# A head's two chunks on the partition halves: new layout, k loaded once, Gram in quarters, placed inverses in two buffers

## The chip, the cores and the metric

One core of a Trainium2 chip runs the whole program. The metric is the device time of one execution in microseconds; the time before is the median of three runs. A span is the part of an execution that the profile covers.

## The reference, cut to what is computed

A delta-rule attention over 4 batches, 8 heads, 768 tokens, head size 48, and two expert layers that take its output. The change touches the attention alone.

```python
k_n = k / (norm(k) + 1e-6)
for t in range(S):                       # state: 48 x 48 per batch and head
    y[t] = q[t] @ state
    state += beta[t] * outer(k_n[t], v[t] - k_n[t] @ state)
x = y as 3072 tokens x 384
x = moe(x, modality bias)                # 8 experts, the best one per token
return moe2(x)                           # 8 experts, 384 tokens each
```

## The kernel before

The tokens are cut into 24 tiles of 128, six per batch. A tile is two chunks of 64 tokens for each of 8 heads, so 16 units of 64 x 64. The recurrence in a chunk becomes a triangular inverse and a few products per unit; between chunks only the state is handed on.

Work per tile runs in three streams that the program orders by hand; each engine works through its own instructions in program order.

- Stage A, eight tiles ahead (`SLOTS = 8`): transposes of k and q (`a_trans`, L208) from the tiles kt and qt, copies to KQ (`a_copy`, ScalarE), Gram products (`a_gram`, L232) into two PSUM tiles pg, the mask times beta (`a_mask`), and the copy of the 32 x 32 diagonal blocks to Dc (`a_diag`). A half of a mask is either four VectorE instructions (L243), or four on ScalarE (L241) and one multiply by the mask on GpSimd (L247). `kbeta` (L198, GpSimd) scales k.
- Stage B, per group of four tiles (`stage_b`): VectorE transposes Dc (L271), inverts the 32 x 32 blocks by 30 substitution steps of a multiply (L282) and an add (L286), and transposes the results to XN (L290) and XTc (L292). It is a generator; `bs(k)` takes k steps of it between other VectorE work, by the tables NB0, NB1, MB and PB.
- Stage C, for tile n: `place` copies the four diagonal quarters of the inverses from XTc to XT (four DMAs on SP, L300), `join1` (L314) and `join2` (L326, copies L329) add the off-diagonal block, `solve` (L343) multiplies k and v, `prod` (L357) and `psub` (L361, VectorE) make the operators Rb, and `chain` (L383) applies them to the state, chunk after chunk, a tile later. `store` sends the result out.

The loop body for tile n runs, in this order: chain(n-1, 0), the masks of tile n+7, qcopy and chain_out, a_diag and kbeta of tile n+7, at every fourth tile a new stage B, at every third the norms of three tiles (`norm_sum`, a square root on ScalarE, `norm_fin`), bs, solve(n), chain(n-1, 1), a_trans(n+8), prod and psub for c = 0, place(n+1), join1(n+1), prod and psub for c = 1, store(n-1), bs, a_gram(n+8, 0), join2(n+1), a_gram(n+8, 1). At the end of every third tile k and v of three tiles are loaded, 10 to 12 ahead.

Before, a partition half holds one head of a pair, and a unit is a head pair in a chunk. The rows of k and v lie in RK, twelve slots; a load of some tiles is eight DMAs (four pairs by two halves, L138). k comes a second time in token order, as kt, for the transposes (L127). There is one XT, a block-diagonal 128 x 128 per unit, so that `place(n+1)` has to follow solve(n).

SP issues nearly all transfers from one queue, in program order; a wait in front of one holds those behind it. The place is:

```python
if n + 1 < NT:
    self.place(n + 1)
    self.join1(n + 1)
...
if n % 3 == 2 and n + 10 < NT:
    self.load_k(n + 10, 3, [self.nc.sync])
    self.load_v(n + 10, 3, [self.nc.sync])
```

In tiles with n % 4 = 0 the masks of the group's last tile are made: the first half on VectorE, the second on ScalarE and GpSimd; its diagonal copies are four ScalarE instructions (L265), and stage B for the group follows at once.

## Time and profile before

| | before |
|---|---|
| time, median of 3 runs | 948.79 us (948.7 to 949.35) |
| profiled execution | 950.61 us, its span 948.70 |
| TensorE busy | 821.5 us, 87% |
| VectorE busy | 641.2 us, 68% |
| ScalarE busy | 445.0 us, 47% |
| GpSimd busy | 282.5 us, 30% |
| mean granted clock of TensorE | 0.941 of full |

In the rows PE is TensorE, PEld its weight loads, DVE VectorE, ACT ScalarE, POOL GpSimd and SPq SyncE's queue of transfers. L300 is line 300 of the kernel before. Busy time of PE is modelled at its ends, so a busy PE is not a PE at its peak. A row of the timeline gives start and length in us, then, in brackets, how long the engine had been idle and what released it.

### The profile page before, as it was taken

To read this page: it belongs to the slowest core of one execution; us is meant where nothing else is said; L and a number is where in the kernel's file an instruction comes from. 1 tells how busy PE (TensorE), PEld (TensorE's weight loads), DVE (VectorE), ACT (ScalarE), POOL (GpSimd) and SP (SyncE) were. 2 spreads that over 40 slices of the span, in tenths; PEclk is the share of its full clock that TensorE was granted. 3 is DMA by queue.
4 is the path that set the end of the run, shared out by engine and by line. 5 is a ranking of instruction groups with operands and counts; after the bars stand their busy time and mean duration, and the time that the engine had idled before them with its cause. 6 is when DMAs were issued, how large, how long until landed. Compare 5 with 4: busy or idle time off the path is not lost. (4 is left out here: it accounts for less than half of the span.)

```text
span 948.7 us, 23825 instructions
## 1 busy us (share of the span) xinstructions
PE 821.5 (87%) x9415; PEld 731.8 (77%) x9415; DVE 641.2 (68%) x1744; ACT 445.0 (47%) x953; POOL 282.5 (30%) x401
## 2 busy tenths in 40 slices
PE   5659759677798886999999999987999999897996
PEld 4548658566687775699999999864778888796996
DVE  4997969787797957665744555227877867776531
ACT  3647647485667556345445554220343243233431
POOL 6254212222221012521122221123363354343411
PEclk9778979797889899999999999999999999998999
DMA  9553345444621115563185431302254235314600
GB/s 157 99 103 59 69 86 93 90 83 78 116 54 37 34 45 167 180 215 125 35 284 184 150 102 43 143 28 92 69 179 161 89 110 176 131 55 166 201 26 28
DMA packets 179402, 102.92 MB, mean 108 GB/s; under 512 B 140838, under 2 KB 161349, under 8 KB 179285
## 3 DMA queue, kind: packets, MB, share of 16 engines
q1 hardware_dynamic: 172564, 81.26, 33.3%
q0 software_dynamic: 6720, 20.07, 6.7%
q8 instruction: 77, 1.26, 0.6%
q14 instruction: 41, 0.33, 0.1%
HBM read 82.36 MB, written 14.55 MB: 102 GB/s over the span
## 5 line engine op out<-in xcount | busy, mean ns | idle before, releaser
L1083 PE MATMUL ph<-xT,HL 128*128 128x384 f32 x1152 | 232.8, 345 | 10.9 <-DVE hh L1091 8.4
L1103 PE MATMUL po<-HL,hh 128*128 128x384 f32 x1152 | 239.3, 346 | 0.2 <-DVE hh L1091 0.2
L1083 PEld LDWEIGHTS ph<-xT,HL 128*128 128x128 f32 x1152 | 202.6, 190 | 21.1 <-DVE hh L1091 10.8
L1103 PEld LDWEIGHTS po<-HL,hh 128*128 128x128 f32 x1152 | 198.0, 189 | 3.1 <-DVE hh L1091 0.5
L1086 ACT ACTIVATE hh<-ph 128x384 fp32r<-128x384 f32 x128 | 62.8, 491 | 183.1 <-PE ph L1083 156.8
L1054 DVE TENSOR_TENSOR HL<-raw,HL 128x768 fp32r<-128x768 f32 x104 | 106.5, 1035 | 56.0 <-ACT HL L1053 55.5
L1091 DVE SCALAR_TENSOR_TENSOR hh<-ph,hh 128x384 fp32r<-128x384 f32 x128 | 70.7, 553 | 80.3 <-ACT hh L1086 69.7
L1053 ACT ACTIVATE HL<-raw 128x768 fp32r<-128x768 f32 x128 | 103.3, 839 | 32.5 <-DMA raw<-in_moe_w_dram 32.4
L282 DVE TENSOR_TENSOR Dtmp<-Dt 128x30 f32<-128x30 f32 (+22 forms) x199 | 81.2, 416 | 3.9
L343 PE MATMUL pz<-RK,XT 64*64 64x96 f32 x768 | 50.2, 284 | 37.9 <-DMA XT<-XTc 36.7
L361 DVE TENSOR_TENSOR R<-pz,C 112x448 f32<-112x448 f32 x96 | 57.2, 615 | 29.7 <-PE pz L357 22.3
L286 DVE TENSOR_TENSOR Dt<-Dt,Dtmp 128x30 f32<-128x30 f32 (+22 forms) x199 | 74.8, 383 | 3.1
L343 PEld LDWEIGHTS pz<-RK,XT 64*64 64x64 f32 x768 | 43.8, 162 | 41.5 <-issue 34.8
L383 PE MATMUL pc<-SI,R 112*48 112x56 f32 (+1 forms) x1536 | 62.5, 234 | 10.8 <-DVE R L361 6.9
L383 PEld LDWEIGHTS pc<-SI,R 112*48 112x48 f32 (+1 forms) x1536 | 55.2, 143 | 18.7 <-DVE R L361 7.4
L1054 POOL TENSOR_TENSOR HL<-raw,HL 128x768 fp32r<-128x768 f32 x24 | 46.7, 1952 | 63.2 <-ACT HL L1053 63.1
L402 POOL COPY xt<-LG 128x8 f32<-128x8 f32 x24 | 5.1, 211 | 189.9 <-issue 77.2
L1141 POOL DMA_INDIRECT x2buf<-x,pidx x24 | 23.8, 993 | 106.0 <-ACT x L1137 86.0
L232 PE MATMUL pa<-KQ 64*64 64x128 f32 x640 | 47.9, 297 | 7.4 <-ACT KQ L221 7.4
L357 PE MATMUL pz<-AT,Z 64*112 64x112 f32 x768 | 50.8, 273 | 3.1 <-ACT Z L347 3.0
L357 PEld LDWEIGHTS pz<-AT,Z 64*112 64x112 f32 x768 | 42.4, 177 | 7.6 <-ACT Z L347 3.0
L232 PEld LDWEIGHTS pa<-KQ 64*64 64x64 f32 x640 | 38.7, 146 | 10.9 <-ACT KQ L221 8.1
(406 smaller groups left out, 1213.7 us busy)
## 6 DMA issues: line engine op xcount, KB each, us to landing
raw<-in_moe_w_dram SPq DMA_DIRECT2D x68, 768.0 KB, 6.0
xbuf<-xt SPq DMA_DIRECT2D x24, 196.0 KB, 1.9
qt<-in_q_dram SPq DMA_DIRECT2D x22, 192.0 KB, 3.9
kt<-in_k_dram SPq DMA_DIRECT2D x21, 192.0 KB, 3.5
RK<-in_k_dram SPq DMA_DIRECT2D x48, 72.0 KB, 2.7
RK<-in_v_dram SPq DMA_DIRECT2D x48, 72.0 KB, 2.7
XT<-XTc SPq DMA_DIRECT2D x92, 32.0 KB, 2.2
Dc<-AT SPq DMA_DIRECT2D x48, 32.0 KB, 1.9
```

What stands on the lines that cost most here:

```text
L232: nc.tensor.matmul(pg[r, p], KQ[:, 0:64], KQ, start=True, stop=True)
L282: nc.vector.tensor_mul(t[:, i:k], X[:, j + 1 + i:j + 1 + k, j:j + 1].to_broadcast([128, k - i, j]), X[:, j:j + 1, :j].to_broadcast([128, k ...
L286: nc.vector.tensor_add(X[:, j + 1 + i:j + 1 + k, :j], X[:, j + 1 + i:j + 1 + k, :j], t[:, i:k])
L343: nc.tensor.matmul(pz[r, p], self.XT[0][r, u, r], self.RK[r, n % RSLOTS, u], start=True, stop=True)
L357: nc.tensor.matmul(self.pr[h][:, p], self.Z[r, u], self.AT[r, n % SLOTS, u, 64:176], start=True, stop=True)
L383: nc.tensor.matmul(self.pc[r, hd], self.Rb[n % 2][0:112, hd % 2, c, hd // 2, r], SI[0:112, hd], start=True, stop=True)
L1053: nc.scalar.activation(t[:, i, 0, c], self.raw[s][i][:, c], AF.Copy)
L1054: (nc.gpsimd if pool else nc.vector).tensor_sub(t[:, i, 1, c], self.raw[s][i][:, c], t[:, i, 0, c].bitcast(F32))
L1083: nc.tensor.matmul(self.ph, W[:, i, a, c], x[:, k, b], start=(k == 0 and n == 0), stop=(k == 2 and n == 2))
L1086: nc.scalar.activation(h[:, 0], self.ph, AF.Relu)
L1091: self.nc.vector.scalar_tensor_tensor(h[:, 1], ph, 0.0, h[:, 0].bitcast(F32), op0=OP.max, op1=OP.subtract)
L1103: nc.tensor.matmul(self.po[s][t], h[:, a, r], W[:, 2 + i, b, c], start=(f == 0 and n == 0), stop=(f == 7 and n == 2))
```

## The change

RK is laid out by token: partition 64c + j is token j of chunk c, and a slot holds k of eight heads, each padded from 48 to 64, and behind them v. So k is loaded once, a tile per DMA, and its slot serves the transposes too; kt goes, qt gets four buffers. beta comes in one DMA. A unit is now a head, its two chunks on the two halves. The two PSUM tiles of Gram belong to the two heads of a pair; each call of `a_gram` makes two head pairs in all four quarters of the array (row half by head, column half by chunk). `psub`'s halves are chunks, so that `chain(n, 0)` reads what both calls of `psub` wrote. XT keeps only the diagonal 64 x 64 of each unit, in two buffers, and `place(n+1)` moves to the start of tile n, unless n % 4 = 3. k and v of tile n + 12 are loaded at the end of every tile. With n % 4 = 0 both halves of the mask are made on VectorE (SPH) and the diagonal copies too (DIA 2, L259). The rest of the diff follows the layout in other access patterns and isn't shown.

```diff
@@ -22,10 +22,11 @@
 NG = 6
 SLOTS = 8
 RSLOTS = 12
+QB = 4
 NB0, NB1 = (7, 8, 8, 30), (3, 6, 0, 3)
 NBT, NBS = 9, 6
 MB, PB = (0, 1, 2, 1), (1, 1, 1, 2)
-SPL, DIA, QO = (0, 0, 1, 0), (0, 3, 3, 3), (0, 1, 1, 1)
+SPL, SPH, DIA, QO = (0, 0, 1, 0), (0, 1, 1, 1), (2, 3, 3, 3), (0, 1, 1, 1)
 WM = (30, 2, 3)
 HB = 60
 NP = (4, 7, 6)
@@ -47,15 +48,16 @@
         self.ps = ctx.enter_context(tc.tile_pool(name="attp", bufs=1, space=PSUM))
         self.ident = consts["ident"]
         self.mask = cA.tile([128, 128], F32, name="mask")
+        self.K = lambda sl, cnt=1: self.RK[:, sl:sl + cnt, 0:512].rearrange("p s (u d) -> p s u d", d=64)
+        self.V = lambda sl, cnt=1: self.RK[:, sl:sl + cnt, 512:896].rearrange("p s (u d) -> p s u d", d=48)
         self.AT = c1.tile([128, SLOTS, 8, 176], F32, name="AT")
-        self.RK = c1.tile([128, RSLOTS, 8, 96], F32, name="RK")
+        self.RK = c1.tile([128, RSLOTS, 896], F32, name="RK")
         self.KQ = c1.tile([128, SLOTS, 4, 2, 128], F32, name="KQ")
-        self.kt = [cA.tile([128, 8, 64], F32, name=f"kt{i}") for i in range(2)]
-        self.qt = [cA.tile([128, 8, 64], F32, name=f"qt{i}") for i in range(2)]
-        self.XT = [c1.tile([128, 8, 128], F32, name=f"XT{i}") for i in range(1)]
-        self.C = [c1.tile([112, 2, 2, 4, 112], F32, name=f"C{i}") for i in range(1)]
+        self.qt = [cA.tile([128, 8, 64], F32, name=f"qt{i}") for i in range(QB)]
+        self.XT = [c1.tile([128, 8, 64], F32, name=f"XT{i}") for i in range(2)]
+        self.C = [c1.tile([112, 2, 8, 112], F32, name=f"C{i}") for i in range(1)]
         self.SI = [c1.tile([128, 8, 56], F32, name=f"SI{i}") for i in range(2)]
-        self.Rb = [c1.tile([128, 2, 2, 4, 112], F32, name=f"R{i}") for i in range(2)]
+        self.Rb = [c1.tile([128, 2, 8, 112], F32, name=f"R{i}") for i in range(2)]
         self.Z = c1.tile([128, 8, 112], F32, name="Z")
         self.bu = c1.tile([128, 192], F32, name="bu")
         self.bp = c1.tile([128, 192], F32, name="bp")
@@ -65,24 +67,18 @@
         for h in range(2):
             nc.gpsimd.iota(it[64 * h:64 * h + 64].rearrange("p (a i) -> p a i", a=2), pattern=[[0, 2], [1, 64]], base=0,
                            channel_multiplier=-1, allow_small_or_imprecise_dtypes=True)
-        bt = self.wa.tile([128, 1024], F32, name="Dc", bufs=1)[:96, :256].rearrange("p (a h j) -> p a h j", a=2, h=2)
-        for i in range(2):
-            nc.vector.memset(self.kt[i][:, :, 48:], 0.0)
+        bt = self.wa.tile([128, 1024], F32, name="Dc", bufs=1)[:96, :256].rearrange("p (a j) -> p a j", a=2)
+        self.load_k(0, 1)
+        nc.gpsimd.dma_start(bt, bass.AP(tensor=beta.tensor, offset=beta.offset, ap=[[128, 96], [96 * 128, 2], [1, 128]]))
+        self.load_q(0)
+        nc.vector.memset(self.K(0, 4)[:, :, :, 48:], 0.0)
+        for i in range(QB):
             nc.vector.memset(self.qt[i][:, :, 48:], 0.0)
-        early = [self.w.tile([128, 32, 32], F32, name=x, bufs=1).rearrange("p u i -> p (u i)").rearrange("p (a h d) -> p a h d", a=2, h=8)
-                 for x in ("XTc", "XN")]
-        for x in early:
-            nc.vector.memset(x[:, :, :, 48:], 0.0)
-        self.early = [(x[:, 0], x[:, 1]) for x in early]
-        self.load_tok(0, nc.gpsimd, 1)
-        for b in range(B):
-            src = bass.AP(tensor=beta.tensor, offset=beta.offset + b * H * S, ap=[[64, 12], [2 * S, 4], [S, 2], [1, 64]])
-            nc.gpsimd.dma_start(bt[(b % 2) * 48:(b % 2) * 48 + 48, b // 2], src)
-        self.load_k(4, 2, [nc.gpsimd])
-        self.load_k(0, 4, [nc.sync])
-        self.load_tok(0, nc.sync, 2)
+        self.load_k(4, 2, nc.gpsimd)
+        self.load_k(1, 3)
         for n in range(1, 4):
-            self.load_tok(n)
+            self.load_q(n)
+        nc.vector.memset(self.K(4, RSLOTS - 4)[:, :, :, 48:], 0.0)
         nc.vector.tensor_scalar(self.mask[:, :64], it[:, :64], 0.0, -1.0, op0=OP.is_gt, op1=OP.mult)
         nc.vector.tensor_scalar(self.mask[:, 64:], it[:, 64:], 0.0, None, op0=OP.is_gt)
 
@@ -103,57 +99,47 @@
...
-    def tok(self, n):
-        return self.early[n - 2] if n in (2, 3) else (self.kt[n % 2], self.qt[n % 2])
-
-    def load_tok(self, n, eng=None, part=3):
-        eng = eng or self.nc.sync
+    def load(self, n, x, t, eng):
+
         b, tt = divmod(n, 6)
-        s = slice(tt * 128, tt * 128 + 128)
-        for t, x in list(zip(self.tok(n), (self.k, self.q)))[part % 2 == 0:2 if part > 1 else 1]:
-            eng.dma_start(t[:, :, 0:48], x[b, :, s, :].rearrange("h s d -> s h d"))
-
-    def load_rows(self, n, cnt, x, o, eng):
-
-        b, tt = divmod(n, 6)
-        sl = n % RSLOTS
-        for p in range(4):
-            for h in range(2):
-                src = bass.AP(tensor=x.tensor, offset=x.offset + ((b * H + 2 * p + h) * S + tt * 128) * D,
-                              ap=[[D, 64], [64 * D, 2 * cnt], [1, D]])
-                dst = self.RK[64 * h:64 * h + 64, sl:sl + cnt].rearrange("p s (c u) d -> p (s c) u d", c=2)[:, :, p, o:o + 48]
-                eng[p * len(eng) // 4].dma_start(dst, src)
-
-    def load_k(self, n, cnt, eng):
-        self.load_rows(n, cnt, self.k, 0, eng)
-
-    def load_v(self, n, cnt, eng):
-        self.load_rows(n, cnt, self.v, 48, eng)
+        (eng or self.nc.sync).dma_start(t, x[b, :, tt * 128:tt * 128 + 128, :].rearrange("h s d -> s h d"))
+
+    def load_q(self, n, eng=None):
+        self.load(n, self.q, self.qt[n % QB][:, :, 0:48], eng)
+
+    def load_k(self, n, cnt=1, eng=None):
+        for i in range(n, n + cnt):
+            self.load(i, self.k, self.K(i % RSLOTS)[:, 0, :, 0:48], eng)
+
+    def load_v(self, n, cnt=1, eng=None):
+        for i in range(n, n + cnt):
+            self.load(i, self.v, self.V(i % RSLOTS)[:, 0], eng)
 
...
@@ -202,15 +188,13 @@
     def a_trans(self, n, tag="pa", bufs=2):
         nc = self.nc
         pp = []
-        for x in self.tok(n):
+        for x in (self.K(n % RSLOTS)[:, 0], self.qt[n % QB]):
             pk = self.ps.tile([128, 4, 128], F32, name=tag, bufs=bufs)
             for p in range(4):
                 nc.tensor.transpose(pk[:, p], x[:, 2 * p:2 * p + 2].rearrange("p h d -> p (h d)"), self.ident)
             pp.append(pk.rearrange("p a (c j) -> p a c j", c=2))
-        if n < 2:
-            self.load_tok(n + 4)
-        elif 3 < n < NT - 2:
-            self.load_tok(n + 2)
+        if n + QB < NT:
+            self.load_q(n + QB)
         self.pp = pp
 
     def a_copy(self, n):
@@ -221,29 +205,31 @@
         nc.scalar.activation(self.KQ[:, sl, :, :, 64:128], pq, AF.Copy)
 
 
-    def a_gram(self, n, c):
-        nc = self.nc
-        tag = ("pm", "pc")[c] if n < SLOTS and n % 2 else "pa"
-        pg = self.pg[n % 2, c] = self.ps.tile([128, 4, 128], F32, name=tag, bufs=2 if tag == "pa" else 1)
-        for p in range(4):
-            for h in range(2):
-                r = slice(64 * h, 64 * h + 64)
-                KQ = self.KQ[r, n % SLOTS, p, c]
-                nc.tensor.matmul(pg[r, p], KQ[:, 0:64], KQ, start=True, stop=True)
-
-    def a_mask(self, n, c, split=False):
+    def a_gram(self, n, k):
+        nc = self.nc
+        if k == 0:
+
+            for i in range(2):
+                tag = ("pm", "pc")[i] if n < SLOTS and n % 2 else "pa"
+                self.pg[n % 2, i] = self.ps.tile([128, 4, 128], F32, name=tag, bufs=2 if tag == "pa" else 1)
+        for p in (2 * k, 2 * k + 1):
+            for i, c in ((0, 0), (1, 1), (0, 1), (1, 0)):
+                KQ = self.KQ[64 * i:64 * i + 64, n % SLOTS, p, c]
+                nc.tensor.matmul(self.pg[n % 2, i][64 * c:64 * c + 64, p], KQ[:, 0:64], KQ, start=True, stop=True)
+
+    def a_mask(self, n, i, split=False):
         nc = self.nc
         A = self.AT[:, n % SLOTS]
         for p in range(4):
-            u = 4 * c + p
+            u = 2 * p + i
             bp = self.bp[:, n * 8 + u:n * 8 + u + 1]
             if split:
-                nc.scalar.activation(A[:, u, 0:128], self.pg[n % 2, c][:, p], AF.Copy, scale=bp)
+                nc.scalar.activation(A[:, u, 0:128], self.pg[n % 2, i][:, p], AF.Copy, scale=bp)
             else:
-                nc.vector.scalar_tensor_tensor(A[:, u, 0:128], self.pg[n % 2, c][:, p], bp, self.mask, op0=OP.mult, op1=OP.mult)
+                nc.vector.scalar_tensor_tensor(A[:, u, 0:128], self.pg[n % 2, i][:, p], bp, self.mask, op0=OP.mult, op1=OP.mult)
                 self.bs(MB[n % 4])
         if split:
-            A = A[:, 4 * c:4 * c + 4, 0:128]
+            A = A[:, i::2, 0:128]
             nc.gpsimd.tensor_mul(A, A, self.mask[:, None, :].to_broadcast([128, 4, 128]))
 
     def a_diag(self, n, pool=True):
@@ -297,9 +283,9 @@
         for qd in range(4):
             r = slice(32 * qd, 32 * qd + 32)
             if n:
-                self.nc.sync.dma_start(self.XT[0][r, :, r], self.XTc[n // 4][r, us])
+                self.nc.sync.dma_start(self.XT[n % 2][r, :, 32 * (qd % 2):32 * (qd % 2) + 32], self.XTc[n // 4][r, us])
             else:
-                self.nc.scalar.activation(self.XT[0][r, :, r], self.XTc[n // 4][r, us], AF.Copy)
+                self.nc.scalar.activation(self.XT[n % 2][r, :, 32 * (qd % 2):32 * (qd % 2) + 32], self.XTc[n // 4][r, us], AF.Copy)
 
 
     def join1(self, n):
@@ -340,7 +326,9 @@
             u = 4 * c + p
             for h in range(2):
                 r = slice(64 * h, 64 * h + 64)
-                nc.tensor.matmul(pz[r, p], self.XT[0][r, u, r], self.RK[r, n % RSLOTS, u], start=True, stop=True)
+                k, v = self.K(n % RSLOTS)[r, 0, u, 0:48], self.V(n % RSLOTS)[r, 0, u]
+                kv = bass.AP(tensor=k.tensor, offset=k.offset, ap=[k.ap[0], [v.offset - k.offset, 2], k.ap[1]])
+                nc.tensor.matmul(pz[r, p], self.XT[n % 2][r, u], kv, start=True, stop=True)
 
     def zcopy(self, c):
         zo = self.Z[:, 4 * c:4 * c + 4]
@@ -380,7 +368,7 @@
         self.pc = self.ps.tile([112, 8, 56], F32, name="pc")
         for hd in range(8):
             for r in (slice(64, 112), slice(0, 64)):
-                nc.tensor.matmul(self.pc[r, hd], self.Rb[n % 2][0:112, hd % 2, c, hd // 2, r], SI[0:112, hd], start=True, stop=True)
+                nc.tensor.matmul(self.pc[r, hd], self.Rb[n % 2][0:112, c, hd, r], SI[0:112, hd], start=True, stop=True)
 
     def chain_out(self, n, c):
         nc = self.nc
@@ -496,6 +484,8 @@
             A = m < NT
             g = n // 4 + 1
             nb, ne = (NB0[n % 4], NB1[n % 4]) if n < 16 else (NBT, NBS)
+            if n % 4 < 3 and n + 1 < NT:
+                self.place(n + 1)
             if Dn:
                 self.chain(n - 1, 0)
             if n == 0:
@@ -504,7 +494,7 @@
                     self.zcopy(c)
             if Dn and m - 1 < NT:
                 self.a_mask(m - 1, 0, SPL[n % 4])
-                self.a_mask(m - 1, 1, True)
+                self.a_mask(m - 1, 1, SPH[n % 4])
             if C and not QO[n % 4]:
                 self.qcopy(n)
             if Dn:
@@ -537,7 +527,8 @@
             if C:
                 self.psub(n, 0)
             if n + 1 < NT:
-                self.place(n + 1)
+                if n % 4 == 3:
+                    self.place(n + 1)
                 self.join1(n + 1)
             if C:
                 self.prod(n, 1)
@@ -557,9 +548,9 @@
                 self.a_gram(m, 1)
             if n > 18:
                 next(side, None)
-            if n % 3 == 2 and n + 10 < NT:
-                self.load_k(n + 10, 3, [self.nc.sync])
-                self.load_v(n + 10, 3, [self.nc.sync])
+            if n + 12 < NT:
+                self.load_k(n + 12)
+                self.load_v(n + 12)
 
 
 E, F, DM, N = 8, 1024, 384, 3072
```

## Rows read from the trace of the kernel before

**Rows 1.** The page, busy us, share of the span and instructions of each engine.
```profile
PE 821.5 (87%) x9415; PEld 731.8 (77%) x9415; DVE 641.2 (68%) x1744; ACT 445.0 (47%) x953; POOL 282.5 (30%) x401
```

**Rows 2.** Windows by stage: busy us per engine, granted clock, DMA share, GB/s.
```profile
0.00:30.85 30.85, 17.11 (x170) 14.56 (x170) 16.55 (x57) 16.16 (x29) 15.59 (x29) 1.00 1.06 141
30.85:71.80 40.95, 22.84 (x212) 20.59 (x212) 40.27 (x120) 20.41 (x59) 17.67 (x14) 0.75 0.59 104
...
84.20:306.20 222.00, 176.76 (x3742) 156.17 (x3738) 181.76 (x447) 143.01 (x360) 54.78 (x59) 0.88 0.42 77
```

**Rows 3.** Waits from 84.2 to 306.2 us: total us, times, longest us.
```profile
PE pz L343 <- DMA XT<-XTc: 33.7, 7, 10.1
...
DVE Dt L271 <- ACT Dc L265: 14.1, 3, 5.3
...
DVE R L361 <- PE pz L357: 10.0, 6, 3.6
DVE nt L176 <- ACT nt L168: 8.9, 5, 3.6
...
DVE XTc L292 <- DMA XT<-XTc: 1.5, 1, 1.5
```

**Rows 4.** Timeline around the solve of tile 4.
```profile
119.72 5.76 SPq L138 DMA_DIRECT2D RK<-in_v_dram  x8
...
123.59 1.12 DVE L243 SCALAR_TENSOR_TENSOR AT<-pa,bp,mask 128x128 f32<-128x128 f32 x4
...
125.58 2.61 SPq L261 DMA_DIRECT2D Dc<-AT  x4
...
127.56 1.69 ACT L265 ACTIVATE Dc<-AT 32x256 f32<-32x256 f32 x4
...
129.55 3.03 SPq L300 DMA_DIRECT2D XT<-XTc  x4
...
133.68 0.55 PE L343 MATMUL pz<-RK,XT 64*64 64x96 f32 x2 [8.75 <-DMA XT<-XTc]
```

**Rows 5.** Windows of tiles 4, 5 and 8; columns as in rows 2.
```profile
123.30:144.40 21.10, 12.35 (x226) 11.05 (x222) 13.68 (x40) 9.95 (x25) 4.36 (x4) 0.76 0.49 85
144.40:155.00 10.60, 10.60 (x257) 9.51 (x251) 10.25 (x27) 8.35 (x22) 2.40 (x3) 1.00 0.42 79
...
186.00:199.00 13.00, 11.87 (x291) 10.39 (x285) 7.38 (x22) 10.67 (x27) 2.24 (x3) 1.00 0.33 63
```

**Rows 6.** Groups of instructions: VectorE's diagonal copies in tile 3 (busy us, mean ns).
```profile
L259 DVE COPY Dc<-AT 32x256 f32<-32x256 f32 x4 | 1.1, 285 | 0.1
```

**Rows 7.** Timeline in tile 5: VectorE beside a GpSimd multiply, and after it.
```profile
148.11 0.97 POOL L198 TENSOR_TENSOR AT<-RK,bp 128x384 f32<-128x384 f32 x1
...
148.43 0.91 DVE L282 TENSOR_TENSOR Dtmp<-Dt 128x228 f32<-128x228 f32 x1
...
149.37 0.40 DVE L286 TENSOR_TENSOR Dt<-Dt,Dtmp 128x228 f32<-128x228 f32 x1
```

**Rows 8.** Timeline of the start, to the first group's transpose.
```profile
8.82 1.29 SPq L127 DMA_DIRECT2D qt<-in_q_dram  x1
...
18.40 1.13 DVE L243 SCALAR_TENSOR_TENSOR AT<-pa,bp,mask 128x128 f32<-128x128 f32 x4 [2.32 <-PE pa L232]
...
25.54 5.08 ACT L265 ACTIVATE Dc<-AT 32x256 f32<-32x256 f32 x12
...
30.85 1.93 DVE L271 STREAM_TRANSPOSE Dt<-Dc 128x1024 f32<-128x1024 f32 x1
```

**Rows 9.** Timeline in tile 5: the first subtraction of psub(5,1), and the next chain.
```profile
153.58 0.62 DVE L361 TENSOR_TENSOR R<-pz,C 112x448 f32<-112x448 f32 x1
...
155.42 1.15 PE L383 MATMUL pc<-SI,R 112*48 112x56 f32 x32
```

More of the change, by code (lines that the diff above doesn't have):

```diff
@@ L105, in beta_rows @@
         for i in range(2):
-            self.nc.tensor.transpose(pb[:, i * 96:(i + 1) * 96], self.bt[:, i].rearrange("p h j -> p (h j)"), self.ident[:96, :96])
-        self.nc.vector.tensor_copy(self.bu, pb)
+            self.nc.tensor.transpose(pb[:, i * 96:(i + 1) * 96], self.bt[:, i], self.ident[:96, :96])
+        self.nc.vector.tensor_copy(self.bu.rearrange("p (b t u) -> p b u t", b=B, u=8), pb.rearrange("p (b u t) -> p b u t", b=B, u=8))
     def late_init(self, w_gate):
@@ L111, in late_init @@
         for t in self.C:
-            nc.gpsimd.tensor_copy(t[0:48].rearrange("p a b h c -> p (a b h) c")[:, :, 64:112],
+            nc.gpsimd.tensor_copy(t[0:48].rearrange("p a u c -> p (a u) c")[:, :, 64:112],
                                   self.ident[0:48, None, 0:48].to_broadcast([48, 16, 48]))
@@ L150, in norm_sq @@
         sq = self.wa.tile([128, 32, 48], F32, name="sq", bufs=1)[:, :8 * cnt]
-        K = self.RK[:, sl:sl + cnt, :, 0:48].rearrange("p s u d -> p (s u) d")
+        q4 = sq.rearrange("p (s u) d -> p s u d", u=8)
+        K = self.K(sl, cnt)[:, :, :, 0:48]
         if n == 0:
-            nc.vector.tensor_mul(sq[:, 0:16], K[:, 0:16], K[:, 0:16])
-            nc.scalar.activation(sq[:, 16:32], K[:, 16:32], AF.Square)
+            nc.vector.tensor_mul(q4[:, 0:2], K[:, 0:2], K[:, 0:2])
+            nc.scalar.activation(q4[:, 2:4], K[:, 2:4], AF.Square)
         else:
-            nc.scalar.activation(sq, K, AF.Square)
+            nc.scalar.activation(q4, K, AF.Square)
         self.sq = sq
@@ L192, in vscale @@
         sl = n % RSLOTS
-        V = self.RK[:, sl:sl + cnt, :, 48:96].rearrange("p s u d -> p (s u) d")
-        nc.gpsimd.tensor_mul(V, V, self.nm[:, cs, None].to_broadcast([128, 8 * cnt, 48]))
+        V = self.V(sl, cnt)
+        nc.gpsimd.tensor_mul(V, V, self.nm[:, cs].rearrange("p (s u) -> p s u", u=8)[:, :, :, None].to_broadcast([128, cnt, 8, 48]))
     def kbeta(self, n):
-        K = self.RK[:, n % RSLOTS, :, 0:48]
+        K = self.K(n % RSLOTS)[:, 0, :, 0:48]
         self.nc.gpsimd.tensor_mul(self.AT[:, n % SLOTS, :, 128:176], K,
@@ L328, in join2 @@
             a, m = slice(64 * h, 64 * h + 32), slice(64 * h + 32, 64 * h + 64)
-            nc.scalar.activation(self.XT[0][a, :, m], px[a], AF.Copy)
+            nc.scalar.activation(self.XT[n % 2][a, :, 32:64], px[a], AF.Copy)
     def qcopy(self, n):
         for h in range(2):
-            self.nc.scalar.activation(self.C[0][0:48, h, :, :, 0:64].rearrange("p c a j -> p a c j"),
+            self.nc.scalar.activation(self.C[0][0:48, :, h::2, 0:64].rearrange("p c a j -> p a c j"),
                                       self.KQ[64 * h:64 * h + 48, n % SLOTS, :, :, 64:128], AF.Copy)
@@ L360, in psub @@
         for h in range(2):
-            self.nc.vector.tensor_sub(self.Rb[n % 2][0:112, h, c], self.pr[h], self.C[0][:, h, c])
+            self.nc.vector.tensor_sub(self.Rb[n % 2][0:112, h, 4 * c:4 * c + 4], self.pr[h], self.C[0][:, h, 4 * c:4 * c + 4])
             self.bs(PB[n % 4])
@@ L438, in go @@
             self.a_gram(1, c)
-        self.load_k(6, 3, [self.nc.sync])
+        self.load_k(6, 3)
         for n in range(L):
@@ L463, in go @@
             if n == 4:
-                self.load_v(0, 4, [self.nc.sync])
+                self.load_v(0, 4)
                 bs(NP[1])
@@ L469, in go @@
                 self.norm_fin(6, 3)
-                self.load_v(4, 2, [self.nc.sync])
-                self.load_v(6, 3, [self.nc.sync])
-                self.load_k(9, 3, [self.nc.sync])
-                self.load_v(9, 3, [self.nc.sync])
+                self.load_v(4, 2)
+                self.load_v(6, 3)
+                self.load_k(9, 3)
+                self.load_v(9, 3)
             if 1 < n < L - 2:
@@ L1757, in bias_of_tokens @@
     nc, ps = tc.nc, a.ps
-    sc = a.Rb[1].rearrange("p a b h c -> p (a b h c)")
+    sc = a.Rb[1].rearrange("p a u c -> p (a u c)")
     raw = sc[:24, 576:832].bitcast(I32).rearrange("n (t w) -> n t w", w=2)
```

## The prediction, made before the result was known

> **What bounds the kernel now.** I read the busy shares first [rows 1]. TensorE has the largest, 87%, but that is a mean over the whole program, and the change touches only the attention. So I read busy time by stretch next [rows 2]. From 30.85 to 71.80 us VectorE is busy 40.27 of 40.95 us: the first substitution (L282, L286) sets that stretch. From 84.2 to 306.2 us, the loop's tiles 1 to 16, nothing is saturated: 222 us, TensorE 176.76, VectorE 181.76. There the waits have to be read [rows 3]. TensorE's largest is 33.7 us before the solves (L343), for the transfers of the placed inverses (L300). VectorE's are 14.1 us before the group's first transpose, for ScalarE's diagonal copies (L265), 10.0 us before the subtractions (L361), for the products, 8.9 us for the square root and 1.5 us for placed transfers that still read the old inverses.
>
> The timeline of tile 4 shows where TensorE's wait comes from [rows 4]. SP's queue issues eight v transfers in 5.76 us, four diagonal copies after them, and only at 129.55 the four placements; the solve starts at 133.68 after an idle 8.75 us. So the placement isn't slow: it stands in line behind SP's many small issues, once in three tiles. A tile without such a wait takes 10.60 us with TensorE busy throughout; tile 4 takes 21.10, and its granted clock is 0.76 [rows 5], between the 1.2 and 2.4 GHz levels, after TensorE had idled.
>
> But VectorE would not allow 10.6 us everywhere. Its busy time is 13.68 us in tile 4 and 10.25 in tile 5. Its order is fixed by the program, so the sixteen tiles can't take less than its 181.76 us plus the waits that stay. **In this stretch I therefore count VectorE's waits and work, not TensorE's 33.7 us.**
>
> **The change, part by part.**
>
> *Loads.* Before, three tiles cost SP sixteen row transfers, about 0.72 us each to issue (5.76 us for eight), and three separate k transfers; after, six transfers, which at the 1.3 us of a large q issue at start [rows 8] are 8 us at the worst, instead of 11.5 us plus three k issues. Placement moves ahead of the diagonal copies, the q load and the store, except in a group's last tile, where the inverses don't exist yet; the second buffer lets it start before the solve has read the first. In front of it on SP stay the previous tile's store and its two loads. Its four issues (3.03 us, [rows 4]) now delay the diagonal copies queued behind them, but these are used only at the group's end. So the long placement stalls go. What VectorE gets from that is the part of its 10.0 us that four stalled tiles caused: I take 9, leaving the short ones; and the 1.5 us. Bounds: 5 to 10 for the first.
>
> *The group's last mask and diagonal on VectorE.* The 14.1 us for ScalarE's diagonal copies go (three groups; in tile 4 the norm's square root hid behind the same copies, longest wait 3.6 us, of which I take 2.7). Sum of waits that go: 9 + 1.5 + 14.1 + 2.7 = 27.3 us. In exchange VectorE does, in each of tiles 4, 8, 12 and 16, four more masks, 1.12 us [rows 4], and four copies at 285 ns, 1.14 us [rows 6]: 2.26, times four is 9.0 us. Nothing hides these where VectorE is last; in tile 8, busy 7.38 us of 13.00 [rows 5], they only bring it level with TensorE. I charge them in full.
>
> *VectorE against GpSimd.* A multiply of VectorE took 0.91 us beside GpSimd's L198, where the add of the same shape took 0.40 alone [rows 7]. In tiles 8, 12 and 16 L198 used to run while VectorE waited; now it meets VectorE's work. Three times 0.5 is 1.5 us. The masks that leave GpSimd can pay some of it back; I give no credit. The Trainium skill, "SBUF — State Buffer", section "SBUF: two separate sides", says the port pair that VectorE and GpSimd share is an exclusive lock, the later one blocked for the whole instruction. By that the charge would be three whole L198 at 0.97 us, 2.9 instead of 1.5, and the forecast 1.4 us later; the row is in keeping with the rule, since most of L198's length was lost.
>
> So tiles 1 to 16 give 27.3 - 9.0 - 1.5 = **16.8 us**, from 222 to about 205.
>
> *Gram in quarters.* Sixteen instructions still stand for each of two calls per tile. How four quarters of the array overlap no row shows; the nearest is the present call, a subset of a TensorE time that fills 10.60 us in tile 5. Between nothing and half of it may go, but VectorE's work covers either; I take nothing. The masks now need both calls, but they come in the next tile after join2.
>
> *First chain half.* Before, chain(n,0) read what psub(n,0) had written; now its second four heads need the first subtraction of psub(n,1). In tile 5 that is the one that starts at 153.58 and takes 0.62; the chain starts at 155.42 [rows 9], so 1.2 us are free. Where VectorE lags, the first four heads can now start one subtraction sooner, which pays for it. I take 0; the far bound is among the rivals.
>
> *Start.* One load of k serves transposes and norms. The q of tile 1 is issued from 8.82 to 10.11 us now [rows 8]. After, it is SP's sixth large load: 0.74 + 6 x 1.3 = 8.5 us, 1.6 sooner. By tile 3, eight loads have gone by 11.1 us where before SP had first issued the eight row loads and then seven more. Masks start at 18.40 after waiting 2.32 us for Gram, and ScalarE's copies end at 30.62, just ahead of the first transpose at 30.85. I take 3.2 us, bounds 0 (the norm's four k tiles share the wires with the two that GpSimd now issues early) and 4.7. VectorE has no slack from 30.85 to 71.80, so a gain at its start is kept. The added memsets of k's padding fall into its wait for k.
>
> *After 306.2 us.* No masks, no Gram, no loads; placement keeps its place in each group's last tile. I take 0, and 0 for the two expert layers, whose work is unchanged and starts sooner.
>
> Total: 16.8 + 3.2 = 20.0 us. The profiled execution took 950.61 us, 948.70 its span and 1.91 around it; it gives 930.6. The median of the runs shown is 948.79, 1.82 below, so the forecast on that scale is **928.8 us**.
>
> **Rivals.**
>
> *A, the waits stay with VectorE.* If TensorE, waiting for VectorE in the long tiles, drops to a clock like tile 4's 0.76 and delivers the products late, the 10.0 us of product waits and the 8.9 of roots remain. What goes is 14.1 + 1.5 - 10.5 = 5.1 us, and 1 to 2 at the start: 942 us. For it: VectorE's busy time differs from tile to tile (13.68, 10.25, 7.38), so TensorE must wait in some. Against: it needs that in tiles where VectorE has nothing else to do before the subtractions.
>
> *B, more goes.* All of the roots' waits too (8.9 instead of 2.7), 4.7 us at the start, and half of the 9.0 hidden in tiles 8 and 12: 20.0 + 6.2 + 1.5 + 4.5 = 32.2, so 916.6 us. Against: the root stands behind the chain's outputs on ScalarE in the other tiles.
>
> *C, slower: the new tie between chain and second product.* If TensorE, in every tile, waits for that subtraction and its substitution steps, the tie costs up to two subtractions with their steps, some 0.8 us each by the rows' 0.62 plus a step, 1.6 x 23 tiles = 37 us: 965.6 us. It decides from 20.0 / 23 = 0.87 us a tile. Against: the 1.2 us free in tile 5, and that VectorE, not TensorE, is late in most tiles.
>
> *D, placement is still late.* If SP holds it behind a store or load that waits, TensorE's 33.7 us stay, and only the diagonals' part and the start remain: about 942, as in A; at worst nothing.
>
> **How the numbers follow.** Forecast 0.63, within 922 to 936 (5 to 10 us for the product waits, 0 to 4.7 at the start). A and D together 0.17; B 0.12; C 0.05; everything given back, 0.03. The range takes in B's and A's centres with a margin for the unknown prices: 914 to 942. A measurement of this kernel can tell about 0.2%, 1.9 us, from no change. Faster holds the forecast, A, B and most of D, 0.89; slower is C and a small share of the rest, 0.06; 0.05 lies between.
>
> **What would show it.** Right: no wait of L343 for L300 above 3 us, except at a group's first tile; no wait of the transpose L271 for ScalarE; L243 with four more calls in tiles 4, 8, 12, 16 and L259 there too; VectorE above 90% busy over tiles 1 to 16, and those in about 205 us; the first transpose near 27.7. Wrong: long waits of the chain for subtractions with VectorE idle before them (C), product or root waits that keep their sums (A), or k and v transfers that norms or solves now wait for.

## The result, and the profile after

The kernel after takes 926.28 us (median of four runs, 923.88 to 928.03) against 948.92 us before; the ratio is 0.9759 [0.9736, 0.9782]. The gain is 22.6 us, 20.0 were forecast. The profiled execution took 925.76 us, its span 923.60; the spans of the two profiled executions differ by 25.1 us, a little more than the medians.

The page after, in the form of [rows 1]:

```profile
PE 800.7 (87%) x9415; PEld 709.4 (77%) x9415; DVE 651.6 (71%) x1776; ACT 433.2 (47%) x922; POOL 270.6 (29%) x387
```

TensorE still has the largest share, still 87%: the page alone doesn't show what happened. The windows do. They are cut at the same marks as [rows 2] (start to the first transpose; the second group's substitution; tiles 1 to 16) and [rows 5] (tiles 4 and 5), with the same columns:

```profile
0.00:27.30 27.30, 13.60 (x170) 11.00 (x170) 16.95 (x58) 16.50 (x31) 10.28 (x19) 1.00 0.94 130
27.30:69.90 42.60, 19.21 (x247) 17.09 (x248) 41.82 (x120) 20.29 (x60) 17.59 (x14) 0.75 0.49 88
...
119.50:136.10 16.60, 10.87 (x258) 9.36 (x253) 15.90 (x48) 8.13 (x21) 3.10 (x3) 0.94 0.33 63
136.10:147.00 10.90, 10.90 (x229) 9.70 (x227) 10.56 (x27) 7.15 (x18) 2.37 (x3) 0.78 0.43 85
...
80.90:283.90 203.00, 165.16 (x3722) 142.96 (x3716) 192.86 (x479) 131.24 (x327) 49.75 (x55) 0.89 0.35 68
```

Tiles 1 to 16 went from 222.0 to 203.0 us, and VectorE is busy for 95% of them, 82% before. The start is 3.56 us shorter (first transpose at 27.29, not 30.85), 3.3 of it still there at tile 1: in between, the second group's substitution takes 1.65 us more (42.60 against 40.95) and tile 0 1.40 less. The rest of the attention went from 61.9 to 60.6, the expert layers from 580.6 to 579.1; the expert layers differ by about that much between executions anyway (578.5 to 582.0 in the runs below).

The waits of tiles 1 to 16 after, in the form of [rows 3]:

```profile
PEld pc L371 <- DVE R L349: 23.8, 20, 4.2
PE pc L371 <- DVE R L349: 20.0, 14, 4.0
...
DVE nt L162 <- ACT nt L154: 2.4, 5, 0.9
...
PE pz L331 <- DMA XT<-XTc: 2.1, 3, 0.9
...
DVE R L349 <- PE pz L345: 1.7, 1, 1.7
```

VectorE's waits fell from 34.5 us to 4.1, and TensorE's 33.7 us for the placed inverses to 2.1. In their place TensorE waits 20.0 us in the chain for VectorE's subtractions (4.0 before). VectorE, which it waits for, is busy for 95% of the stretch, so this is what an engine with slack looks like; e4 below gives TensorE more work there, and the loop stays as it is.

The timeline around the solve of tile 4, to set against [rows 4]:

```profile
119.80 2.15 DVE L229 SCALAR_TENSOR_TENSOR AT<-pa,bp,mask 128x128 f32<-128x128 f32 x8
...
120.73 0.44 SPq L118 DMA_DIRECT2D RK<-in_k_dram  x1
121.22 0.70 SPq L118 DMA_DIRECT2D RK<-in_v_dram  x1
...
121.72 1.48 PE L331 MATMUL pz<-RK,XT 64*64 64x96 f32 x30 [1.14 <-ACT lgr L379]
...
121.97 2.73 SPq L286 DMA_DIRECT2D XT<-XTc  x4
121.99 1.18 DVE L245 COPY Dc<-AT 32x256 f32<-32x256 f32 x4
...
125.05 1.95 DVE L257 STREAM_TRANSPOSE Dt<-Dc 128x1024 f32<-128x1024 f32 x1
```

Two loads of 0.44 and 0.70 us stand where eight of 5.76 stood. The placement issued here, at 121.97, is already that of tile 5, while tile 4 is being solved from the other buffer. VectorE makes eight masks and four diagonal copies in a row; only the norm's sum and the step behind its root come before the group's transpose, which has no wait of its own.

### The profile page after: what moved, and what is told of

Read it like the earlier page. It is cut to its first block, busy times and chain, and to the rows that moved or that the text cites. A ratio compares the mean times of both kernels' runs of the same rounds, so it can differ in the third digit from the quotient of the medians.

```text
span 923.6 us, 23619 instructions
## 1 busy us (share of the span) xinstructions
PE 800.7 (87%) x9415; PEld 709.4 (77%) x9415; DVE 651.6 (71%) x1776; ACT 433.2 (47%) x922; POOL 270.6 (29%) x387
## 4 chain that ended last, share of the span: by engine, by line
PE 42%; DVE 32%; issue 10%; DMA 7%; ACT 4%; POOL 3%; SPq 1%; DVEq 0%; POOLq 0%; ACTq 0%
PE ph L1074 14%; PE po L1094 14%; DVE Dtmp L268 7%; DVE Dt L272 6%; DVE R L349 4%; DMA raw<-in_moe_w_dram 2%; PE pr L1340 2%; DMA xg<-x2buf,lidx 2%; DVE HL L1045 2%; PE pz L345 2%; PE ph L713 1%; PE pz L331 1%; POOL out_dram L1600 1%; PE pt L1060 1%; PE pc L371 1%
## 5 line engine op out<-in xcount | busy, mean ns | idle before, releaser
L1074 PE MATMUL ph<-xT,HL 128*128 128x384 f32 x1152 | 231.4, 344 | 11.3 <-DVE hh L1082 8.4
L371 PE MATMUL pc<-SI,R 112*48 112x56 f32 (+1 forms) x1536 | 65.5, 238 | 26.9 <-DVE R L349 23.0
L268 DVE TENSOR_TENSOR Dtmp<-Dt 128x30 f32<-128x30 f32 (+22 forms) x199 | 84.8, 434 | 3.9
L371 PEld LDWEIGHTS pc<-SI,R 112*48 112x48 f32 (+1 forms) x1536 | 57.2, 146 | 36.5 <-DVE R L349 26.0
L1045 POOL TENSOR_TENSOR HL<-raw,HL 128x768 fp32r<-128x768 f32 x24 | 46.9, 1962 | 62.8 <-ACT HL L1044 62.7
L345 PEld LDWEIGHTS pz<-AT,Z 64*112 64x112 f32 x768 | 43.6, 182 | 10.9 <-ACT Z L335 6.3
L1600 POOL DMA_INDIRECT out_dram<-x,oid x24 | 25.7, 1069 | 58.0 <-ACT x L1597 48.3
L378 ACT ACTIVATE SI<-pc 48x448 f32<-48x448 f32 x44 | 23.7, 540 | 38.9 <-PE pc L371 38.5
```

Source lines behind the costliest of these rows:

```text
L268: nc.vector.tensor_mul(t[:, i:k], X[:, j + 1 + i:j + 1 + k, j:j + 1].to_broadcast([128, k - i, j]), X[:, j:j + 1, :j].to_broadcast([128, k ...
L345: nc.tensor.matmul(self.pr[h][:, p], self.Z[r, u], self.AT[r, n % SLOTS, u, 64:176], start=True, stop=True)
L371: nc.tensor.matmul(self.pc[r, hd], self.Rb[n % 2][0:112, c, hd, r], SI[0:112, hd], start=True, stop=True)
L1045: (nc.gpsimd if pool else nc.vector).tensor_sub(t[:, i, 1, c], self.raw[s][i][:, c], t[:, i, 0, c].bitcast(F32))
L1074: nc.tensor.matmul(self.ph, W[:, i, a, c], x[:, k, b], start=(k == 0 and n == 0), stop=(k == 2 and n == 2))
```

## The experiments

V is the prediction's theory: the loop (tiles 1 to 16) lasts as long as VectorE's work plus VectorE's own waits, whatever TensorE waits for. The other letters are rivals of the single experiment. Ratios are against runs of the kernel before on the same chip. This table is read from the windows and waits of each profiled execution, in us; the last column is TensorE's, the four before it VectorE's.

| | loop | busy | wait for diagonals | for products | for roots | solve for XT |
|---|---|---|---|---|---|---|
| before | 222.0 | 181.76 | 14.1 | 10.0 | 8.9 | 33.7 |
| after | 203.0 | 192.86 | 0 | 1.7 | 2.4 | 2.1 |
| e0 after again | 203.3 | 192.71 | 0 | 2.2 | 2.4 | 1.2 |
| e7 before, early placement | 212.0 | 181.43 | 14.1 | 0.8 | 9.6 | 21.9 |
| e8 before, masks moved | 217.4 | 191.29 | 0 | 10.8 | 6.5 | 35.0 |
| e1 after, masks back | 207.4 | 184.87 | 10.7 | 0 | 4.5 | 3.3 |
| e6 after, diagonals back | 203.2 | 188.01 | 5.3 | 1.4 | 2.8 | 0.7 |
| e2 after, late placement | 203.1 | 192.72 | 0 | 1.8 | 2.4 | 6.0 |
| e3 after, many loads | 199.6 | 190.18 | 0 | 0.4 | 2.8 | 13.4 |
| e10 after, both | 206.0 | 190.79 | 0 | 5.9 | 2.8 | 27.6 |
| e4 after, Gram twice | 203.3 | 192.72 | 0 | 0 | 3.6 | 0.2 |
| e9 after, all kbeta moved | 206.1 | 187.61 | 0 | 2.0 | 8.5 | 2.8 |
| e11 after, some kbeta moved | 201.3 | 189.34 | 0 | 3.5 | 2.4 | 0.7 |
| e12 after, e11 and v's scaling | 198.3 | 189.84 | 0 | 0.5 | 1.9 | 1.5 |

Busy time and waits, the few small ones that the table leaves out included, fall short of each loop by 5.7 to 6.3 us, gaps between VectorE's own instructions. That the parts add up is bookkeeping, and would hold for any engine; what tells is which edits moved the sum. Each row is one execution. e11 and e12 run the same instructions in the loop and differ by 3.0 us there, so a difference of about 3 us between two rows shows nothing by itself.

**e0, the kernel after once more**, beside e7, e9 and e10.

> The changed kernel itself, run beside the others of this call so that they have it on the same chip. Every theory: 924 to 929, the loop's tiles 1 to 16 in 203 us.

927.26 us (926.51 to 928.57), ratio 0.9766 [0.9747, 0.9785]. The result repeats.

**e7, the kernel before with early placement alone.**

```diff
-        self.XT = [c1.tile([128, 8, 128], F32, name=f"XT{i}") for i in range(1)]
+        self.XT = [c1.tile([128, 8, 128], F32, name=f"XT{i}") for i in range(2)]
...
+            if n % 4 < 3 and n + 1 < NT:
+                self.place(n + 1)
             if Dn:
                 self.chain(n - 1, 0)
...
-                self.place(n + 1)
+                if n % 4 == 3:
+                    self.place(n + 1)
```

> The kernel before with the second buffer and the early placement alone; loads, layout, Gram, masks and diagonals as they were. Theory V: the four long waits before the solves shrink from 8.8 to 10.1 us to 3 to 6, most of the 10.0 us that VectorE waited for products goes, the 14.1 us for ScalarE's diagonals stay and the start stays: 7 to 10 us faster, 939 to 942. Rival D (SP's line holds the placement however early it is issued): 946 to 949. Rival F (TensorE's waits are the bound): most of its 33.7 us goes, 920 to 930.

940.09 us (938.51 to 942.84), 0.9906 [0.9887, 0.9926]. V's range held. The loop lost 10.0 us. Its waits:

```profile
PE pz L343 <- DMA XT<-XTc: 21.9, 9, 4.9
...
DVE Dt L271 <- ACT Dc L265: 14.1, 3, 5.3
...
DVE R L361 <- PE pz L357: 0.8, 3, 0.4
```

VectorE's product waits went from 10.0 to 0.8 and the 1.5 us at XTc went altogether, 10.7 in all; 0.7 more for roots and 0.4 for Gram came, which leaves 9.6, and the loop gained 10.0. TensorE still waits 21.9 us for placement. Counted by TensorE, one would have looked for 11.8 (33.7 - 21.9), not far off here; the two ways of counting part in e3.

**e8, the kernel before with the group's last mask and diagonals on VectorE alone.**

```diff
-SPL, DIA, QO = (0, 0, 1, 0), (0, 3, 3, 3), (0, 1, 1, 1)
+SPL, SPH, DIA, QO = (0, 0, 1, 0), (0, 1, 1, 1), (2, 3, 3, 3), (0, 1, 1, 1)
...
-                self.a_mask(m - 1, 1, True)
+                self.a_mask(m - 1, 1, SPH[n % 4])
```

> The kernel before with the group's last mask and diagonal copies on VectorE, alone. Theory V: the 14.1 us that the transposes waited and 2.7 us of the root's wait go, 10.5 us of work and contention come: 5 to 7 us faster, 942 to 944. From the changed kernel, where moving the two back cost 4.4 us in tiles 1 to 16, 3 to 5 us are to be expected: 945 to 947. Rival W (VectorE's work is what counts): 9 to 11 us slower, 958 to 961.

945.59 us (941.23 to 948.53), 0.9948 [0.9931, 0.9966]: 3.5 us faster than the kernel before on its chip. That is within the 3 to 5 us that e1, further down, had led me to expect, and short of V's own range, 942 to 944. The loop lost 4.6 us: 14.1 of diagonals and 2.4 of roots gone, 9.5 of work added, product waits up by 0.8. The two parts alone give 10.0 + 4.6 = 14.6 of the 19.0 us; no run isolates the other 4.4.

**e1, the kernel after with that half mask and the diagonals back on ScalarE and GpSimd.**

```diff
-SPL, SPH, DIA, QO = (0, 0, 1, 0), (0, 1, 1, 1), (2, 3, 3, 3), (0, 1, 1, 1)
+SPL, SPH, DIA, QO = (0, 0, 1, 0), (1, 1, 1, 1), (0, 3, 3, 3), (0, 1, 1, 1)
```

> The changed kernel, with the group's last mask half back on ScalarE and GpSimd and its diagonal copies back on ScalarE, as before. Theory V (the tiles 1 to 16 are set by VectorE's work and its waits): VectorE's busy time there falls from 192.9 by about 9 to 11 us, but the transpose waits for ScalarE's diagonal copies again, 4 to 5 us in each of three tiles, and the root in tile 4 by some 2.5; the span grows by 4 to 8 us, to 930 to 934. Rival W (only VectorE's amount of work counts, the waits would be taken up elsewhere): 9 to 11 us less on the busiest engine makes it faster, 916 to 918.

930.67 us (926.62 to 931.79), 0.9783 [0.9755, 0.9811]; V's range held. The loop is 4.4 us longer: VectorE works 8.0 less and waits 10.7 for diagonals and 2.1 more for roots. So this part of the change takes on eight microseconds of work and saves thirteen of waiting. The times alone would not show it, their ratios to the kernel before overlap (0.9783 here, 0.9759 for the kernel after).

**e6, only the diagonals back on ScalarE**, the masks stay.

```diff
-SPL, SPH, DIA, QO = (0, 0, 1, 0), (0, 1, 1, 1), (2, 3, 3, 3), (0, 1, 1, 1)
+SPL, SPH, DIA, QO = (0, 0, 1, 0), (0, 1, 1, 1), (0, 3, 3, 3), (0, 1, 1, 1)
```

> The changed kernel with the group's last diagonal copies back on ScalarE, the last mask still on VectorE. Theory V: VectorE does 4 x 1.15 us less, but the first transpose waits for four ScalarE copies (1.69 us) that start when the masks end; in tile 4 the norm's sum hides them. Tiles 1 to 16 within 2 us of 203, the time 925 to 928. Rival W (only the amount of VectorE's work counts): 4.6 us less, 922 to 923. Rival M (of the two, the diagonals carried the whole price of moving the mask back): 930 to 932.

927.44 us (925.5 to 929.23), 0.9781 [0.9764, 0.9797]. The loop is unchanged, 203.2. One exchange, priced exactly: VectorE works 4.85 us less and waits 5.3 for the same copies.

**e2, placement late in every tile**, with the two buffers and the single loads kept.

```diff
-            if n % 4 < 3 and n + 1 < NT:
-                self.place(n + 1)
...
-                if n % 4 == 3:
-                    self.place(n + 1)
+                self.place(n + 1)
```

> The changed kernel, with the placement of the next tile's inverses always at its old place, after the first product; the second buffer stays. Theory V with the line on SP as the cause of the old stalls: the loads are now 2 short issues per tile, so the line is short without the early place too; at most 1 us of wait in a tile before the solve and 0 to 3 us in all, 926 to 929. Rival P (the early place is what removed the stalls): four or more waits of several us for the placed transfers come back, 936 to 946.

926.04 us (924.12 to 929.17), 0.9741 [0.9714, 0.9769]: no loss. V's range held, though TensorE's wait is somewhat longer than expected (6.0 us in nine waits, up to 1.8 at once); with few issues on SP, placement needn't be early.

**e3, sixteen row loads in every third tile again**, the placement stays early.

```diff
+    def load_rows(self, n, cnt, x, view):
+        b, tt = divmod(n, 6)
+        for h in range(8):
+            self.nc.sync.dma_start(view(n % RSLOTS, cnt)[:, :, h, 0:48],
+                                   x[b, h, tt * 128:(tt + cnt) * 128, :].rearrange("(s p) d -> p s d", p=128))
...
-            if n + 12 < NT:
-                self.load_k(n + 12)
-                self.load_v(n + 12)
+            if n % 3 == 2 and n + 10 < NT:
+                self.load_rows(n + 10, 3, self.k, self.K)
+                self.load_rows(n + 10, 3, self.v, self.V)
```

> The changed kernel, with k and v loaded for three tiles at a time in eight transfers each (one per head), sixteen issues on SP at the end of every third tile, as many as before; early placement and second buffer stay. Theory V with the line on SP as the cause: in one tile of three the placement stands behind about 11 us of issues, the solve waits 3 to 6 us for it, four times, of which VectorE passes on a part: 6 to 14 us slower, 932 to 940. Rival P (early place and second buffer suffice): no more than 2 us, 926 to 928.

A miss for V: 925.66 us (920.99 to 932.23), 0.9751 [0.9713, 0.979], no loss, as rival P had it. The stall did come, VectorE just didn't feel it:

```profile
PE pz L337 <- DMA XT<-XTc: 13.4, 8, 5.5
...
DVE R L355 <- PE pz L351: 0.4, 1, 0.4
```

TensorE waits 13.4 us, up to 5.5 at once, and its products are still in time. My expectation had passed the stall on to VectorE, against my own rule. The loop is even 3.4 us shorter: VectorE works 2.7 us less for the same instructions. Which overlap became cheaper is not settled, and the times, spread over 11 us, don't show a gain.

**e10, late placement and many loads together**, the two edits above.

> The changed kernel with both: placement late in the tile and k and v in sixteen issues every third tile, so that only the second buffer is left of what shortens the way of the placed inverses. Each edit alone left tiles 1 to 16 at 203 and 200 us. Theory V (a wait on TensorE costs only what it exceeds TensorE's slack by; the line on SP is cured by either edit): the solves of four tiles wait 7 to 10 us again, VectorE waits for the products again by 6 to 9 us, tiles 1 to 16 take 209 to 212 us, the time is 932 to 936. Rival B (the second buffer alone cures it): no wait above 6 us, 925 to 928. Rival S (VectorE takes up waits of any length): waits as in V, but the time stays at 925 to 928.

929.23 us (926.34 to 932.29), 0.9784 [0.9761, 0.9806], below V's range; the ratio overlaps that of e0 on the same chip, 0.9766. TensorE waits 27.6 us for placement, up to 8.2 at once, so rival B fails. But VectorE waits only 5.9 us for products, 1.7 to 2.2 in the kernel after. The direction was right in the waits, the size too large; the loop's 3.0 us more are no more than two executions of one loop can differ by. So either remedy, fewer issues or an earlier place, suffices to keep the products in time; without both, the second buffer and the changed rest still leave VectorE 4.1 us less product wait than before.

**e4, the Gram products made twice** (the same numbers written again).

```diff
-        for p in (2 * k, 2 * k + 1):
+        for p in (2 * k, 2 * k + 1) * 2:
```

> The changed kernel, with every Gram product made twice (the second overwrites the first with the same values), so that TensorE's Gram takes about as long as before the change, 1 us more per tile. Theory V: TensorE has 38 of 203 us idle in tiles 1 to 16 and VectorE is last: at most 2 us, 926 to 928. Rival T (the shorter Gram is part of the gain): about 1 us in each of 16 tiles and in the eight before the loop, 15 to 24 us slower, 941 to 950.

929.15 us (928.06 to 930.78), 0.9775 [0.9747, 0.9803], above V's 926 to 928 and far from rival T. In the loop nothing: 203.3, though TensorE is busy 7.9 us more. But the first transpose comes at 30.28 instead of 27.29. The first Gram in the kernel before:

```profile
16.38 3.68 PE L232 MATMUL pa<-KQ 64*64 64x128 f32 x32
```

The timeline of the start in the kernel after:

```profile
14.33 1.98 PE L218 MATMUL pa<-KQ 64*64 64x128 f32 x32
...
16.37 2.16 DVE L229 SCALAR_TENSOR_TENSOR AT<-pa,bp,mask 128x128 f32<-128x128 f32 x8
```

The same stretch in this kernel:

```profile
14.18 3.71 PE L218 MATMUL pa<-KQ 64*64 64x128 f32 x64
...
17.93 2.16 DVE L229 SCALAR_TENSOR_TENSOR AT<-pa,bp,mask 128x128 f32<-128x128 f32 x8 [1.82 <-PE pa L218]
21.38 1.13 DVE L229 SCALAR_TENSOR_TENSOR AT<-pm,bp,mask 128x128 f32<-128x128 f32 x4 [1.29 <-PE pc L218]
...
24.31 2.16 DVE L229 SCALAR_TENSOR_TENSOR AT<-pa,bp,mask 128x128 f32<-128x128 f32 x8 [0.77 <-PE pa L218]
...
30.28 1.96 DVE L257 STREAM_TRANSPOSE Dt<-Dc 128x1024 f32<-128x1024 f32 x1 [0.53 <-ACT KQ L205]
```

With 64 products in quarters the first Gram takes what 32 in two quarters took before, VectorE waits 1.82 us for it, where 2.32 stood in [rows 8], and for the next ones too, and 3.0 of the start's 3.56 us are gone. So without the shorter Gram that gain doesn't come. It isn't Gram's alone: in the kernel after, Gram also begins 2.05 us sooner (14.33 against 16.38). I had expected at most 2 us here, and not at the start.

**e9, kbeta on ScalarE** from tile 4 on, to see what GpSimd's multiplies cost VectorE.

```diff
     def kbeta(self, n):
         K = self.K(n % RSLOTS)[:, 0, :, 0:48]
+        if n > 3:
+            for u in range(8):
+                self.nc.scalar.activation(self.AT[:, n % SLOTS, u, 128:176], K[:, u], AF.Copy, scale=self.bp[:, n * 8 + u:n * 8 + u + 1])
+            return
```

> The changed kernel with k times beta (L184 on GpSimd, one instruction a tile) made by eight ScalarE instructions from tile 4 on. Theory V with the port that VectorE and GpSimd contend for: each L184 costs VectorE about 0.5 us in tiles 1 to 16 and in four tiles ahead of the loop, so 7 to 10 us less on the engine that is last: 916 to 920. Rival Q (ScalarE, in order, with 1.7 us more per tile hands the state and the solved rows to TensorE later, and VectorE then waits for products): no gain or up to 5 us slower, 926 to 931.

925.2 us (921.52 to 926.17), 0.9733 [0.9711, 0.9756]; V missed by 5 us, and the time lies between the two expectations. VectorE works 5.25 us less in the loop, but in every third tile ScalarE's eight new instructions stand ahead of the square root in program order, and VectorE's waits for roots grow by 6.1 us. Products, which rival Q named, come no later than before (2.0 us). The loop is 3.1 us longer, with 1.6 us of new waits for Gram in it. Ahead of the loop the second transpose comes 3.6 us sooner (66.3 instead of 69.9).

**e11, kbeta on ScalarE only in some tiles**: 4 to 7, which are made ahead of the loop, and those made in seven of its tiles that have no root.

```diff
+        if 3 < n < 8 or n in (9, 10, 12, 13, 18, 21, 22):
```

This line stands in place of `if n > 3:`.

> The changed kernel with k times beta on ScalarE only where no root and no group's start stands on ScalarE in the same tile (tiles 4 to 7 ahead of the loop; in the loop tiles 2, 3, 5, 6, 11, 14, 15), on GpSimd elsewhere. All of it on ScalarE gave 3.4 us ahead of the loop and took 2.8 in it, where the root's waits grew from 2.4 to 8.5 us. Theory V: the 3.4 us stay, and 2 to 3 come in the loop: 920 to 923. Rival Q (ScalarE's order costs in those tiles too): 923 to 927.

916.8 us (915.63 to 920.82), 0.9661 [0.9645, 0.9677], better than V's range: this version beats both kernels, the one after by 9.5 us between the medians. Its profiled execution took 920.82, the longest of the five. It shows 3.1 us up to tile 1, 1.7 in the loop and 1.7 in the rest of the attention, against 1.9 more in the expert layers; the root's waits stay at 2.4. So the trace accounts for about half of the 9.5 us, and where the other executions got the rest isn't shown.

**e12, e11 with the scaling of v of tiles 0 to 3 on ScalarE as well** (32 small instructions in place of GpSimd's one, behind the diagonals of tile 7).

```diff
+        if n == 0:
+            for s in range(cnt):
+                for u in range(8):
+                    i = (n + s) * 8 + u
+                    nc.scalar.activation(V[:, s, u], V[:, s, u], AF.Copy, scale=self.nm[:, i:i + 1])
+            return
         nc.gpsimd...
...
-        self.vscale(0, 4)
         self.a_diag(7, DP[7])
+        self.vscale(0, 4)
```

> The kernel of the run before this one, with the first scaling of v (four tiles, one GpSimd instruction of 2.75 us ahead of the loop) made by 32 ScalarE instructions in the 11.5 us that ScalarE is idle there. Theory V with contention: one pair of VectorE adds took 4.35 us beside it where such a pair takes 0.45 alone; 2 to 4 us less than without this edit, 917 to 921, the second group's transpose at about 63 us. Rival: VectorE's long add is not due to that instruction, no change: 920 to 923.

918.86 us (916.02 to 920.94), 0.9694 [0.9677, 0.971]: in V's range, but the 2 to 4 us that V saw in this edit didn't come, the median is 2.1 above e11's. The timeline in e11 of the multiply that stands beside GpSimd's:

```profile
57.92 2.97 DVE L272 TENSOR_TENSOR Dtmp<-Dt 128x108 f32<-128x108 f32 x1
58.00 2.75 POOL L180 TENSOR_TENSOR RK<-RK,nm 128x1536 f32<-128x1536 f32 x1
```

The same multiply in e12:

```profile
56.77 0.27 DVE L278 TENSOR_TENSOR Dtmp<-Dt 128x108 f32<-128x108 f32 x1
...
58.33 7.32 ACT L184 ACTIVATE RK<-RK,nm 128x48 f32<-128x48 f32 x32
```

The 2.7 us come back at once, and the second transpose moves to 62.7 from 66.5 (this execution was 1.1 us ahead before that multiply). But ScalarE's 7.32 us stand ahead of the copies of join1, and by the end of tile 0 only 1.0 of the 3.8 us is left (76.8 against 77.8).

## Why the prediction was right, and where it was not

**The bound, right.** The loop follows VectorE's work and waits, and the signs named for it came: no wait of the solve for placement above 0.9 us, none of the transpose for ScalarE, VectorE 95% busy. Taking 11.8 us of TensorE's wait away gave 10.0 because 9.6 of VectorE's went with it (e7); putting 11.3 back cost nothing where VectorE's did not return (e3); doubling Gram cost the loop nothing (e4). Rival A is refuted by the table, and its clock step too: tile 5 now has a granted clock of 0.78, tile 4 of 0.94, the other way round than in [rows 5], and tile 5 still takes 10.9 us (10.60 before). D is refuted by the 2.1 us.

**The terms of the sum.** Forecast 27.3 us of waits gone and 10.5 of work and contention added, so 205; measured 30.4 and 11.1, and 203.0. By term: diagonals 14.1, exact; products 8.3 where I took 9; XT 1.5, exact; roots 6.5 where I took 2.7, the one mis-sized term. I counted the root in tile 4 alone. Its wait there went from 3.56 us to 0.29, so 3.27, and the four other norms, which I had left as they were, went from 5.3 to 2.1. For tile 4 I named the diagonal copies on ScalarE. The wait for its root in e6, with these copies back, and then in e1, with the mask's half back as well:

```profile
123.88 0.18 DVE L162 TENSOR_SCALAR nt<-nt 128x24 f32<-128x24 f32 x1 [0.74 <-ACT nt L154]
```

```profile
124.11 0.18 DVE L162 TENSOR_SCALAR nt<-nt 128x24 f32<-128x24 f32 x1 [2.74 <-ACT nt L154]
```

So most of it was the mask's half on ScalarE, not the copies. The other four stay short in e1 (1.8 us) and long in e8 (6.2), so it is not this part of the change that freed them; which one did was not separated.

**Work charged in full, right.** 9.0 us for masks and copies; e8 added 9.5 and e1 removed 8.0. Contention with GpSimd at 1.5 fits what remains, 11.1 - 9.0 = 2.1, though no run isolates it in the tiles where I charged it. Moving the same multiply off GpSimd took 3.5 us of VectorE's work away for seven of them (e11) and 5.25 for sixteen (e9), 0.5 and 0.3 us each; but VectorE's work also fell by 2.7 us in e3, which moved none.

**The start, right in size, with a step that failed.** 3.56 us came where I said 3.2, but I credited the loads alone and took nothing for Gram in quarters. The step that failed is "VectorE's work covers either": it doesn't at the start, where [rows 8] showed VectorE waiting 2.32 us for Gram. With Gram at its old length only 0.57 of the 3.56 us are left (e4). The sooner start of Gram, which I had in the loads, is needed too: 1.98 us from 16.38 on would end at 18.36, and the first mask began at 18.40 already before (an estimate from these rows). No run has the quarters with the old loads, so how the 3.56 us divide is open, and that the size came out near is luck. Nor was the gain simply kept behind it: VectorE's work in the second group's substitution grew by 1.55 us (41.82 against 40.27), and tile 0 gave 1.40 back; why isn't shown. In the loop the zero for Gram was right.

**Placement, right but overdetermined.** I described early placement and fewer issues as one remedy; e2 and e3 show either alone does it.

**C.** TensorE's wait for subtractions rose to 20.0 us, the sign I had named for C, but without an idle VectorE, so the tie costs nothing that these traces show; no run isolates it.

## What to carry to other kernels

Before you price a stall, find the engine with the most work in the stretch (here VectorE, 181.76 us against TensorE's 176.76) and sum its own waits: a stall of another engine is worth only what it passes on. Then test the choice by edits, since busy time and waits add up for any engine. An edit that gains nothing in a steady loop can still pay where the pipeline fills, so look at each edit once in the loop and once at the start. And moving a small operation off an engine that slows the bound one may pay, if nothing urgent stands behind it in its new queue (e11 against e9).
